# Token runs of 32 in place of 33, seven products in twelve up groups, closing sums given to DMA, and the root chain moved to GpSimd in a fused convolution and MLP kernel

## The chip, the cores and the metric

One core of one Trainium2 chip. The metric is device time in microseconds (us). Each kernel was run several times, and medians are quoted. All runs used here are of the fast state: their granted clocks are given where they matter. The result was measured in one session (the record does not name its chip) and the experiments on three other chips; in the four places the kernel before took 992.5, 996.2, 995.7 and 995.4 us. So kernels are compared by their ratio to the kernel before on the same chip, not by their microseconds.

## The reference

Softmax weights over 7 taps and 8 heads make a causal depthwise convolution, and its result y goes through a layer norm without shift, a product up to 768 features, a ReLU, a product down to 192, and a residual addition. All is float32.

```python
# x: (8, 4224, 192); weight: (8 heads, 7 taps); w_ch1: (192, 768); w_ch2: (768, 192)
w = softmax(weight, axis=-1)
y[b, s, h, :] = sum_k w[h, k] * x_padded[b, s + k, h, :]        # causal, 24 channels a head
yn = (y - mean(y)) / sqrt(var(y) + 1e-06) * g_ln
out = y + maximum(yn @ w_ch1, 0.0) @ w_ch2
```

## The kernel before

Tokens lie on the 128 partitions in *runs*: 33 tokens of one batch entry per partition. A *group* is some columns of these runs (17 and 16 alternately, 6 to 12 in the first entry). Per group, ScalarE and DVE convolve, DVE transposes, TensorE multiplies up and down in 32x32 tiles, and the output is transposed back, scaled by the root (1/sqrt of the variance) on ScalarE, and added to y in HBM by an accumulating DMA. The *down* product uses seven products for eight quarters (as in Strassen's scheme) from the fourth group on; the *up* product does so only in the groups of 16 (`MIXED`).

```python
    R = S // P                        # 33 tokens a run
    J = 17
    ...
    groups = []
    for b in range(B):
        j0 = 0
        for n in (6, 7, 8, R - 21) if b == 0 else (J - 1, J):
            groups.append((b, j0, n))
            j0 += n
    MIXED = range(6, NG, 2)           # six groups, all of 16
    ...
    def root(g):                      # 16 operations, all on DVE
        nc.vector.tensor_tensor(d, st[:, 0:n, 1], st[:, 0:n, 4], op=ALU.subtract)
        nc.vector.tensor_tensor(v, st[:, 0:n, 2], st[:, 0:n, 5], op=ALU.add)
        ...
        for _ in range(3):
            nc.vector.tensor_tensor(d, r, r, op=ALU.mult)
            ...
    def sums_of_y(g):                 # the four sums that the seven products of the up need
        nc.vector.tensor_tensor(s1, a21, a22, op=ALU.add)
        nc.vector.tensor_tensor(s2, s1, a11, op=ALU.subtract)
        nc.vector.tensor_tensor(s3, a21, a11, op=ALU.subtract)
        nc.vector.tensor_tensor(s4, a12, s2, op=ALU.subtract)
    ...
    def down_fast(g):                 # ends like this
        product(0, a[:, 1, 1], w2sums[:, 1], c21, False)
        some_taps(taps_behind[4])     # taps of group g+2 on ScalarE, then y += tb by DMA
        product(0, a[:, 0, 0], w2sums[:, 0], parts[1], False)
        some_taps(taps_behind[5])
        product(0, a[:, 0, 1], b[3], c12, False)
    ...
    def finish_fast(g, half, flat, cs, parts):
        fresh = cs[:, CH * half : CH * half + CH, 1]
        nc.vector.tensor_tensor(fresh, fresh, parts[half], op=ALU.add)      # closing sum, DVE
        for c in range(CH * half, CH * half + CH):
            nc.vector.transpose(ot[:, 0:n, C * c : C * c + C], ...)
    ...
        parts = down_fast(g)
        for half in range(last, 2):
            finish_fast(g, half, *parts)
        ...
        if g + 1 in MIXED:
            sums_of_y(g + 1)
```

## Time and profile before

| | before |
|---|---|
| median of device time | 992.5 us |
| span of the profile, granted clock | 992.1 us, 1.00 |
| busy: TensorE, DVE, ScalarE, GpSimd | 99, 89, 59, 8% |
| GpSimd's DMA queue, share of 16 engines | 34.2% |
| first large product starts | 25.9 us |

The prediction below shows the main lines of the page (the profiler's summary of a run), TensorE's timeline and the stretches. Two more places are needed later. First DVE's timeline at the end of a down (start, duration, engine, line, operation): the closing sums, L790, and behind each the three transposes of its half (of the second half, two are shown).

```profile
562.53 0.95 DVE L790 TENSOR_TENSOR cs<-cs,part 128x768 f32<-128x768 f32 x1
563.52 1.90 DVE L792 STREAM_TRANSPOSE ot<-cs 128x512 f32<-128x512 f32 x3
565.34 0.92 DVE L790 TENSOR_TENSOR cs<-cs,ht 128x768 f32<-128x768 f32 x1
566.36 1.31 DVE L792 STREAM_TRANSPOSE ot<-cs 128x512 f32<-128x512 f32 x2
```

None of these rows shows an idle time in brackets: nothing is waited for here, and the sums cost DVE 1.9 us a group. Second, the head of ScalarE's timeline, where the load of the second group is waited for, briefly (brackets: idle before, and what ended it).

```profile
20.43 0.76 ACT L367 ACTIVATE y<-xg,taps 128x168 f32<-128x168 f32 x2 [0.45 <-DMA xg<-in_x_dram]
```

### The profile page before, as it was taken

The numbers are of one execution on the slowest core, as the hardware profiler recorded it, in microseconds if no ns is written. First come the engines' busy times: TensorE is split into PE (matmuls) and PEld (weight loads), VectorE is DVE, ScalarE is ACT, GpSimd is POOL, SyncE is SP. The second block draws the span as 40 slices with busy tenths as digits, with TensorE's granted clock in tenths as the row PEclk, the third lists the DMA queues.
The fourth block names the chain that finished last, engine by engine and source line by source line (L and its number), as shares of the span: only waits on it lengthen the run. The fifth ranks groups of instructions, "written<-read, shape, count | busy, mean of one in ns | idle before, by whom it ended". The sixth has DMA issues, their size and how long they took to land.

```text
span 992.1 us, 37342 instructions
## 1 busy us (share of the span) xinstructions
PE 979.3 (99%) x16914; PEld 701.4 (71%) x16914; DVE 886.4 (89%) x1622; ACT 588.9 (59%) x1243; POOL 81.5 (8%) x110
## 2 busy tenths in 40 slices
PE   7999999999999999999999999999999999999997
PEld 5888675578585775858767686666857678585786
DVE  6999998899999998998899988999989999899507
ACT  6536464646577565765658566575666746574451
POOL 2001101000010000101001101010000100010000
PEclk9999999999999999999999999999999999999999
DMA  6254727633738354563636735377273854444031
GB/s 196 90 190 75 207 35 219 195 79 60 227 60 229 92 149 136 101 214 70 213 70 118 224 71 188 76 175 193 38 225 68 213 124 101 98 82 74 2 66 70
DMA packets 18702, 126.88 MB, mean 128 GB/s; under 512 B 2415, under 2 KB 3183, under 8 KB 13678
## 3 DMA queue, kind: packets, MB, share of 16 engines
q0 software_dynamic: 12096, 66.75, 34.2%
q1 hardware_dynamic: 6142, 57.73, 15.1%
q8 instruction: 132, 2.16, 0.9%
q14 instruction: 28, 0.23, 0.1%
q10 hardware_dynamic: 304, 0.00, 0.0%
HBM read 38.95 MB, written 50.23 MB: 90 GB/s over the span
## 4 chain that ended last, share of the span: by engine, by line
PE 94%; issue 2%; DMA 2%; DVE 1%; ACT 0%; SPq 0%; POOL 0%; ACTq 0%; DVEq 0%; POOLq 0%
PE ps L520 48%; PE ps L724 39%; PE ps L671 5%; DMA ht<-parts 1%; DMA room<-in_moe_w_ch_dram 1%; DVE ht L689 1%; PE ps L300 1%; PE ps L325 0%; PE ps L330 0%; ACT parts L596 0%; DVE y L829 0%; PE ps L309 0%; PE ps L312 0%; DVE room L225 0%; DVE room L217 0%
## 5 line engine op out<-in xcount | busy, mean ns | idle before, releaser
L520 PE MATMUL ps<-yt,w 32*128 32x256 f32 (+6 forms) x6624 | 426.6, 412 | 0.6 <-ACT parts L596 0.5
L520 PEld LDWEIGHTS ps<-yt,w 32*128 32x128 f32 x6624 | 331.4, 185 | 91.9 <-issue 52.2
L394 DVE SCALAR_TENSOR_TENSOR y<-xg,taps,y 128x408 f32<-128x408 f32 (+5 forms) x734 | 365.9, 575 | 14.6 <-DMA y<-tb 8.6
L724 PE MATMUL ps<-ht,w2sums 128*32 128x256 f32 (+2 forms) x4320 | 236.9, 377 | 0.0
L689 DVE TENSOR_TENSOR ht<-ht 128x1088 f32<-128x1088 f32 (+2 forms) x162 | 184.5, 1208 | 54.5 <-ACT part L730 26.8
L724 PEld LDWEIGHTS ps<-ht,w2sums 128*32 128x32 f32 x4320 | 140.4, 110 | 90.9
L724 PE MATMUL ps<-ht,w 128*32 128x256 f32 (+2 forms) x3240 | 182.6, 378 | 0.2 <-issue 0.2
L508 ACT ACTIVATE ht<-ps 128x256 f32<-128x256 f32 (+2 forms) x312 | 100.9, 409 | 95.6 <-PE ps L520 95.6
L724 PEld LDWEIGHTS ps<-ht,w 128*32 128x32 f32 x3240 | 103.8, 110 | 74.6 <-ACT ot L817 4.6
L730 ACT COPY cs<-ps 128x256 f32<-128x256 f32 (+2 forms) x180 | 65.1, 371 | 120.0 <-PE ps L724 120.0
L510 ACT ACTIVATE ht<-ps 128x2048 f32<-128x2048 f32 (+5 forms) x48 | 63.4, 1320 | 65.0 <-PE ps L520 65.0
L817 ACT ACTIVATE ot<-ot,r 128x192 f32<-128x192 f32 x247 | 94.6, 458 | 4.9 <-DVE ot L792 4.9
L367 ACT ACTIVATE y<-xg,taps 128x408 f32<-128x408 f32 (+5 forms) x137 | 70.5, 588 | 5.9 <-DVE st L421 5.3
L421 DVE BATCH_NORM_STATS2 st<-y 128x6 f32<-128x192 f32 x264 | 70.0, 341 | 0.0
L792 DVE STREAM_TRANSPOSE ot<-cs 128x512 f32<-128x512 f32 (+2 forms) x90 | 58.3, 686 | 8.3 <-ACT cs L730 6.3
L380 ACT ACTIVATE tb<-xg,taps 128x384 f32<-128x384 f32 (+1 forms) x112 | 60.8, 616 | 0.0
L821 POOL DMA_DIRECT2D out_dram<-ot x34 | 31.6, 945 | 347.3 <-ACT ht L508 178.6
L405 DVE STREAM_TRANSPOSE yt<-y 128x3072 f32<-128x3072 f32 (+5 forms) x19 | 56.2, 2957 | 1.9
L671 PE MATMUL ps<-ht,w 128*32 128x192 f32 (+3 forms) x1152 | 51.4, 339 | 0.0
L520 PE MATMUL ps<-ysums,w1sums 32*128 32x256 f32 x864 | 47.7, 374 | 0.0
L671 PEld LDWEIGHTS ps<-ht,w 128*32 128x32 f32 x1152 | 37.1, 110 | 13.7 <-issue 0.5
L383 POOL DMA_DIRECT2D y<-tb x28 | 24.9, 1050 | 264.4 <-ACT cs L730 141.5
(104 smaller groups left out, 499.6 us busy)
## 6 DMA issues: line engine op xcount, KB each, us to landing
y<-tb POOLq DMA_DIRECT2D x21, 768.0 KB, 6.1
out_dram<-ot POOLq DMA_DIRECT2D x20, 768.0 KB, 6.7
xg<-in_x_dram SPq DMA_DIRECT2D x6, 2208.0 KB, 16.1
xg<-in_x_dram SPq DMA_DIRECT2D x6, 2112.0 KB, 12.5
out_dram<-y SPq DMA_DIRECT2D x6, 1632.0 KB, 6.5
out_dram<-y SPq DMA_DIRECT2D x6, 1536.0 KB, 8.0
ht<-parts POOLq DMA_DIRECT2D x6, 1024.0 KB, 7.6
y<-tb POOLq DMA_DIRECT2D x7, 864.0 KB, 10.9
```

What stands on the lines that cost most here:

```text
L367: nc.scalar.mul(dst, src, tap)
L380: nc.scalar.mul(tb[g][:, 0:n, cs], xg[g][:, 1 : 1 + n, cs], taps[:, h, 1:2])
L394: nc.vector.scalar_tensor_tensor(out=y[g][:, 0:n, cs], in0=t[:, k : k + n, cs], scalar=taps[:, h, k : k + 1], in1=y[g][:, 0:n, cs], op0=AL ...
L421: nc.vector.bn_stats(out=sums[g][:, j, :], in_=y[g][:, j, :])
L508: nc.scalar.activation(dst[:, q], src[:, q], AF.Relu)
L510: nc.scalar.activation(dst, src, AF.Relu)
L520: nc.tensor.matmul(banks[:, q, i * w : i * w + w], right[rows, c, P * i : P * i + P], left[rows, :, c, :], start=(first and c == 0 and i = ...
L671: nc.tensor.matmul(bank[C * q : C * q + C, 0:w], w2[:, f, C * c : C * c + C], t[:, f, q, js.start - fast[g] : js.stop - fast[g], :], start ...
L689: nc.vector.tensor_tensor(a[:, *dst, f], a[:, *left, f], a[:, *right, f], op=op)
L724: nc.tensor.matmul(dst[C * q : C * q + C, 0:w], right[:, f, C * c : C * c + C], left[:, f, q], start=(first and f == 0), stop=(f == FC - 1 ...
L730: nc.scalar.copy(to[:, c], dst[:, 0:w].rearrange("p (j t) -> p j t", t=t))
L817: nc.scalar.mul(ots[g][:, j, :], ots[g][:, j, :], rstd[g][:, j : j + 1])
```

## The change

The intent is to use the seven products in the up of twelve groups rather than six (matmuls are the bound), which needs groups of 16 and so runs of 32 tokens. The 128 tokens that remain at each sequence end become one group of 8, loaded as eight small transfers. DVE is relieved to make room: the closing sums of the down become accumulating DMAs in GpSimd's queue, the late product of the up as well, and the root chain goes to GpSimd. The four sums of y become a generator, so that they can be placed between other work: the first two after the transposes of the first half, the third after those of the second.

```diff
-    R = S // P
-    J = 17
+    J = 16
+    R = 2 * J
+    LEFT = (S - P * R) * B // P
...
+    groups = [(0, 0, 6), (None, 0, LEFT), (0, 6, J - 5), (0, J + 1, J - 1)]
+    groups += [(b, j0, J) for b in range(1, B) for j0 in (0, J)]
-    MIXED = range(6, NG, 2)
+    MIXED = range(5, NG - 1)
...
+        if b is None:                          # the group of 8: one transfer a batch entry
+            for b in range(B):
+                queue.dma_start(out=flat[LP * b : LP * b + LP, ...], in_=...)
...
-        nc.vector.tensor_tensor(d, st[:, 0:n, 1], st[:, 0:n, 4], op=ALU.subtract)
+        nc.gpsimd.tensor_tensor(d, st[:, 0:n, 1], st[:, 0:n, 4], op=ALU.subtract)
...  # the whole root chain, 19 operations on GpSimd in place of 16 on DVE
+        def close_by_dma(c, part):
+            add_by_dma(*(v.rearrange("p c j t -> p c (j t)") for v in (c, part)))
...
         product(0, a[:, 1, 1], w2sums[:, 1], c21, False)
+        if g in MIXED:
+            close_by_dma(c21, parts[0])
         some_taps(taps_behind[4])
         product(0, a[:, 0, 0], w2sums[:, 0], parts[1], False)
+        if g in MIXED:
+            close_by_dma(c22, parts[1])
...
-        fresh = cs[:, CH * half : CH * half + CH, 1]
-        nc.vector.tensor_tensor(fresh, fresh, parts[half], op=ALU.add)
+        if g not in MIXED:
+            fresh = cs[:, CH * half : CH * half + CH, 1]
+            nc.vector.tensor_tensor(fresh, fresh, parts[half], op=ALU.add)
...
+        later = sums_of_y(g + 1) if g + 1 in MIXED else iter(())
+        if not last:
+            finish_fast(g, 0, *parts)
+            next(later, None)              # s1 and s2
+        finish_fast(g, 1, *parts)
+        next(later, None)                  # s3; the fourth follows inside the up
```

The order of the products inside the up changed too (the full-width products go last), and so did the places of scalings and convolution steps. Line numbers move: L520, L724, L790 and L792 of before are L532, L734, L802 and L806 of after.

## The prediction

> **What bounds the kernel now.** I read the page's busy shares first, then the TensorE timeline, then the stretches of two groups, then the DMA issues.
>
> ```profile
> span 992.1 us, 37342 instructions
> PE 979.3 (99%) x16914; PEld 701.4 (71%) x16914; DVE 886.4 (89%) x1622; ACT 588.9 (59%) x1243; POOL 81.5 (8%) x110
> ...
> PE 94%; issue 2%; DMA 2%; DVE 1%; ACT 0%; SPq 0%; POOL 0%; ACTq 0%; DVEq 0%; POOLq 0%
> ```
>
> TensorE is busy 99% and is 94% of the chain that ended last, so the kernel lasts as long as its matmuls, and only matmuls removed, or new gaps between them, move the time. DVE at 89% is close behind and must be priced too. The timeline (start, duration) of one batch entry, a group of 17 runs with the plain first matmul and then one of 16 with seven products in it:
>
> ```profile
> 449.32 33.28 PE L520 MATMUL ps<-yt,w 32*128 32x256 f32 x576
> ...
> 511.55 10.61 PE L520 MATMUL ps<-yt,w 32*128 32x512 f32 x144
> 521.99 7.95 PE L520 MATMUL ps<-ysums,w1sums 32*128 32x256 f32 x144
> ...
> 567.52 33.28 PE L520 MATMUL ps<-yt,w 32*128 32x256 f32 x576
> ```
>
> No row in between shows an idle gap. From start to start: plain up (17 runs) 33.2 us, its down 29.0, seven-product up (16 runs) 28.64, its down 27.33; 118.2 us per batch entry. Other engines in the same four stretches (columns: PE, PEld, DVE, ACT, POOL busy, clock, DMA share, GB/s):
>
> ```profile
> 449.32:482.54 33.22, 33.22 (x580) 29.43 (x577) 30.14 (x69) 19.32 (x61) 1.95 (x3) 1.00 0.41 75
> 482.54:511.55 29.01, 29.01 (x508) 16.27 (x505) 25.82 (x39) 16.06 (x37) 2.15 (x3) 1.00 0.72 211
> 511.55:540.19 28.64, 28.64 (x436) 22.04 (x432) 26.87 (x43) 22.17 (x25) 3.51 (x4) 1.00 0.46 85
> 540.19:567.52 27.33, 27.33 (x508) 16.28 (x504) 26.68 (x35) 18.41 (x38) 2.42 (x3) 1.00 0.66 200
> ```
>
> The DMA share averages 0.56 over these 118 us. That has room, but the change fills it.
>
> **What the Trainium skill says.** "GPSIMD Engine Reference", section "Performance versus the Vector engine": GpSimd takes about twice DVE's time for a two-input elementwise operation (4497 against 2293 ns at 2048 elements). The trace before has no such operation on GpSimd, so it neither agrees nor not; its 128x128 memsets take about 0.2 us. "SBUF — State Buffer", section "Who interferes with whom": a DVE instruction with two SBUF inputs and a GpSimd instruction that reads SBUF block each other for a whole instruction. No run yet shows it here. "DMA: Bandwidth & Descriptors", section "Two DMAs through the same engine are not ordered": within one queue descriptors start in order. The trace agrees: three GpSimd transfers issued at 649.5, 650.4 and 651.0 us (512, 512, 768 KB) land 4.7, 7.1 and 11.2 us after their issues, each behind the one ahead, at some 190 GB/s in all.
>
> **The change part by part.**
>
> TensorE. One pass at 256 columns costs 15.75/288 = 54.7 ns, at 512 columns 31.12/288 = 108.1 ns: 1.3 ns plus 0.2086 ns a column. The new order on TensorE is known from the build: groups of 6, 8, 11, 15, 16, then twelve of 16 with seven products, then the last of 16 as 11 plus 5. A new seven-product up has the same matmuls as now (336 passes of 256 and 96 of 512), only in another order. So:
> - 6 runs: 13.04 + 11.84 = 24.9 (as now)
> - 8 runs: 15.75 + 15.68 = 31.4
> - 11 runs: 2 x 288 x 74.7 ns = 43.0
> - 15 runs: 288 x 101.4 ns + 504 x 50.9 ns = 54.8
> - 16 plain: 31.12 + 27.33 = 58.5
> - twelve of 16: 12 x 55.97 = 671.6
> - last: 288 x (74.7 + 34.7) ns + 504 x 37.5 ns + 9.96 = 60.4
>
> Sum 944.6. Before the first of these lie 25.9 us (weights), after the last matmul 5.2 us. Total **975.7 us**, 16.4 us or 1.65% less than the span. That is the ceiling of the gain and it already falls short of 2%: six more groups save about 3.2 us each, and the runs split off as a group of 8 and the less even early groups take a little back.
>
> DVE, per seven-product group of 16, from busy time over count in the groups table: 40 convolution steps x 0.534 = 21.3; transpose of y 3.4; 16 moments x 0.265 = 4.2; 12 sums on the hidden tile 13.9; 3 additions from PSUM 1.1; 6 transposes out 3.9; 4 sums of y 3.8. Sum 51.6 of 56.0 us, 92%. Gone per group: the addition of the late product (2.4), the closing sums (1.9) and, every other group, the root chain (16 x 0.2 = 3.2). So DVE alone does not become the bound, but it has only 4.4 us per group to lose.
>
> ScalarE: 7 evictions and 2 plain ones x 1.88, 2 ReLUs x 1.9, 16 scalings x 0.38, 18 copies x 0.36, 16 taps x 0.54 = 42 of 56 us. In the up part it holds about 27 of 28.6 us, as it does now with 14 scalings.
>
> DMA, per group: 1 MB three times (was one and two halves in every other group), 384 KB twice (new), taps and output 1.5 MB each, all accumulating, 7.1 MB at about 197 GB/s = 36 us; loading x and storing y 3.7 MB at about 370 GB/s = 10 us. Together 46 of 56 us, **82% against 56%**. This is the part that can turn the gain back.
>
> GpSimd: 19 small operations per two groups, estimated at 0.3 us each from the 0.2 us memsets plus a wait, some 6 us, in the last 3 us of a down and the first few of the next up. First use is the scaling about 10 us into that up. Not on the path if the estimate holds.
>
> Head: x of the second group now comes in 8 transfers of 16 partitions. SyncE issues take about 0.45 us each, and ScalarE waits 0.45 us for this load already; its convolution on DVE is 1.2 us longer than for 7 runs while DVE was ready only 0.8 us early. About +1 us.
>
> **The wait I expect.** Take a down's start as zero. The fifth product is evicted at 20.1, its closing transfer goes out then; the taps end at 21.2 and their two 768 KB transfers follow; the sixth product is evicted at 23.9 and its closing transfer goes out last in the same queue. The trace has such a pair of 768 KB moving data for 8.2 us:
>
> ```profile
> y<-tb POOLq DMA_DIRECT2D x2, 768.0 KB, 8.2
> ```
>
> So 384 + 1536 + 384 KB from 21.4 end near 33.5 and land near 34, which is 6.7 us into the next up. DVE then has the second half's three transposes (2.0) and, behind them in its order, the third sum of y (0.95), ready at about 9.7. TensorE wants that sum for its fourth product at 3 x 2.59 = 7.8. That is **2 us of TensorE idle** at each of the 11 boundaries between seven-product groups, 22 us in all. I give this a half chance: the landing has to come only 2 us sooner for it to vanish, and the code looks as though its author had placed the sums around these waits. Half of 22 is 11: 975.7 + 1 + 11, about **987 us** on the clock of the medians.
>
> **Rivals.** (a) All is hidden; TensorE stays gapless and the time is 976 to 978. For it: 99% busy now, and the one gap of the trace before is 0.53 us. Against it: the queue above. (b) The boundary wait is real and about 2 to 3 us: 997 to 1008, so the whole gain is lost or more. For it: the arithmetic of the queue. (c) The reuse of one buffer inside an up: the first 1 MB transfer must land before the sixth product is evicted, 15.6 us into the up, and goes out at 7.2; 7.6 us of landing is its median, 9.2 its worst, so 1 us is to spare. If GpSimd's root chain is slowed by DVE's two-input operations to 0.7 us an operation, the transfer goes out late at every other group, ScalarE stands, and TensorE loses 2 to 4 us six times: another 12 to 24 us. For it: the port rule. Against it: DVE waits for a transfer, not computing, for much of that time. (d) DVE becomes the bound through the lower sum, which waits for the third 1 MB transfer (landing estimated at 28 us into an up) and leaves under 1 us before the hidden sums are due; 2 us later would cost up to 2 us a group.
>
> **Range and chances.** (a) about 0.4, (b) with or without parts of (c) and (d) about 0.5, worse about 0.1. The range is 975 to 1006. Faster by over 2% means under 972.6, below the TensorE sum: 0.05. Slower by over 2% means above 1012.3: needs over 3 us of idle at every boundary: 0.08. Within 2%: 0.87.
>
> **What would show each step.** TensorE: rows of the seven-product groups 28.6 and 27.3 us long; if start to start exceeds 56 us, the surplus is idle time. Boundary wait: TensorE idle ahead of the matmuls on ysums and w1sums released by DVE, and DVE idle ahead of its output transposes released by the small closing DMA; neither there means (a). Buffer reuse: ScalarE idle ahead of evictions into parts, released by DMA. GpSimd: duration from the chain's first to last operation near 6 us. DMA share near 0.8 in mid-kernel. The prediction is wrong if TensorE's own time per pass changes, if GpSimd's chain takes over 12 us, or if the closing transfers overtake the taps' transfers.

## The result

The changed kernel takes 1041.5 us (1040.7 to 1042.9, 4 runs) against 992.5: **4.9% slower**, where half a per cent faster had been predicted; ratio 1.0494 with a 95% interval of 1.0476 to 1.0512. Ratios here are the mean time of one kernel's fast runs over that of the other's of the same rounds, so not quite the ratio of the quoted medians. The result is outside the predicted range of 975 to 1006 us, and 54 us over the predicted time.

The page of the changed kernel:

```profile
span 1041.2 us, 35698 instructions
PE 987.3 (95%) x16050; PEld 690.0 (66%) x16050; DVE 842.5 (81%) x1465; ACT 625.1 (60%) x1034; POOL 188.6 (18%) x329
...
q0 software_dynamic: 24256, 100.97, 50.6%
...
PE 55%; issue 17%; DMA 14%; DVE 7%; POOL 4%; ACT 1%; POOLq 0%; DVEq 0%; ACTq 0%
```

TensorE has 5% fewer instructions and yet 8 us more busy time, which is a first hint at its clock. Its share of the chain that ended last fell from 94 to 55%; DMA has 14%. DVE was indeed relieved, from 89 to 81%. GpSimd's queue moves half as much again, 101 against 67 MB.

TensorE's timeline over one boundary between two seven-product groups (the down ends and the up starts at 545.67):

```profile
545.67 5.46 PE L532 MATMUL ps<-yt,w 32*128 32x256 f32 x96
550.96 2.77 PE L532 MATMUL ps<-ysums,w1sums 32*128 32x256 f32 x48
557.07 7.15 PE L532 MATMUL ps<-ysums,w1sums 32*128 32x256 f32 x96 [3.35 <-DVE ysums L584]
564.02 2.80 PE L532 MATMUL ps<-yt,w1sums 32*128 32x256 f32 x48
```

Two things are to be seen. Ahead of the fourth product TensorE idles 3.35 us for L584, the third sum of y on DVE. And the 96 passes after it take 7.15 us, where 96 passes of the same shape took 5.46 at the top. The other engines at the same place:

```profile
538.70 1.28 POOL L590 DMA_DIRECT2D cs<-part  x1 [15.14 <-ACT cs L740]
539.72 2.08 POOL L403 DMA_DIRECT2D y<-tb  x2
...
542.59 1.27 POOL L590 DMA_DIRECT2D cs<-room  x1 [0.78 <-ACT room L740]
...
554.19 1.90 DVE L806 STREAM_TRANSPOSE ot<-cs 128x512 f32<-128x512 f32 x3 [7.13 <-DMA cs<-room]
...
556.01 0.92 DVE L584 TENSOR_TENSOR ysums<-yt 128x768 f32<-128x768 f32 x1
```

The second closing transfer, `cs<-room`, is issued at 542.59 behind the two tap transfers of 768 KB; DVE idles 7.13 us for it, transposes, and only then computes the sum that TensorE wants. (Of the twelve such waits of DVE the profile puts seven down to this transfer and five to ScalarE's eviction into `parts_tb`, which ends at the same time, at 554.07 here. e9 below parts the two: there the transfer lands early, and at one boundary DVE transposes at 554.37, where that eviction starts only at 562.54.) The waits, summed over the kernel (engine, operand, line <- releaser: us, times, longest):

```profile
PE ps L532 <- DVE ysums L584: 37.8, 11, 3.8
```

The DMA issues (KB each, median us from issue to landing) show what the place in the queue does; the first of the two equal closing transfers goes ahead of the taps, the second behind them:

```profile
y<-tb POOLq DMA_DIRECT2D x28, 768.0 KB, 9.5
...
cs<-part POOLq DMA_DIRECT2D x12, 384.0 KB, 4.4
cs<-room POOLq DMA_DIRECT2D x12, 384.0 KB, 11.5
```

Stretches around the same boundary (columns: PE, PEld, DVE, ACT and POOL busy, granted clock, DMA share, GB/s; in short stretches the share can come out above 1). The last row is a narrower cut of the first two, from 557.30 to 560.70 us:

```profile
557.07:559.00 1.93, 1.93 (x20) 1.93 (x24) 1.93 (x5) 0.00 (x0) 0.00 (x0) 0.56 1.17 242
559.00:561.00 2.00, 2.00 (x26) 2.00 (x25) 2.00 (x5) 0.00 (x0) 0.00 (x0) 0.57 0.81 164
561.00:563.00 2.00, 2.00 (x44) 2.00 (x43) 2.00 (x4) 1.31 (x1) 0.00 (x0) 1.00 0.03 8
...
557.30:560.70 3.40, 3.40 (x36) 3.40 (x36) 3.40 (x8) 0.00 (x0) 0.00 (x0) 0.50 0.94 193
```

The 0.56 and 0.57 are means over stretches in which the clock changes. The narrower cut has exactly 0.50, and cut into steps of 0.1 us the trace has 0.50 from 557.29 to 560.70, which is 3.41 us, and 1.00 on both sides. The kernel before has 1.00 from its first matmul to its last. At half the clock for 3.41 us, 1.7 us of work is lost, which explains 7.15 us in place of 5.46. One of the eleven boundaries, the first, is spared although its idle time is among the longest:

```profile
313.27 5.46 PE L532 MATMUL ps<-ysums,w1sums 32*128 32x256 f32 x96 [3.67 <-DVE ysums L584]
```

The Trainium skill, "TensorE: Matmul & The Clock Gate", section "What's actually happening", says that an idle window of about 3.4 us takes the clock to half, that about 3.4 us of sustained work bring it back, and that the window runs freely. The trace agrees in the half, in the 3.41 us and in the free running; how idle a window must be is taken up at the end.

The head, ScalarE's timeline:

```profile
26.40 0.80 ACT L387 ACTIVATE y<-xg,taps 128x192 f32<-128x192 f32 x2 [4.83 <-DMA xg<-in_x_dram]
```

The second group's eight small loads land late, ScalarE waits 4.83 us for them (0.45 before), its next work, the evictions of the weights, is late, and the first large product starts at 31.06 rather than 25.90 us.

The account, on the predicted sum of TensorE, head and tail:

| | us |
|---|---|
| predicted sum, no idle time | 975.7 |
| head, 31.06 − 25.90 | 5.2 |
| wait ahead of the second group's up | 0.7 |
| 11 boundaries: the twelve seven-product groups take 730.16 (244.90 to 975.06) less the predicted 671.6 | 58.5 |
| sum, against a span of 1041.2 | 1040.1 |

That is 5.32 us a boundary. At the boundary shown, 3.52 are the wait (the fourth product starts 6.11 us after the third, where 2.59 is a product's time without a wait) and 1.77 the slow clock (the next two products take 6.95 from start to start, where two of 2.59 are due).

### The profile page after: what moved, and what is told of

Its sections match the earlier page's. It is cut to its first block, busy times and chain, and to the rows that moved or that the text cites. A ratio compares the mean times of both kernels' runs of the same rounds, so it can differ in the third digit from the quotient of the medians.

```text
span 1041.2 us, 35698 instructions
## 1 busy us (share of the span) xinstructions
PE 987.3 (95%) x16050; PEld 690.0 (66%) x16050; DVE 842.5 (81%) x1465; ACT 625.1 (60%) x1034; POOL 188.6 (18%) x329
## 4 chain that ended last, share of the span: by engine, by line
PE 55%; issue 17%; DMA 14%; DVE 7%; POOL 4%; ACT 1%; POOLq 0%; DVEq 0%; ACTq 0%
PE ps L532 30%; PE ps L734 21%; DMA cs<-room 9%; PE ps L681 4%; DVE y L414 2%; DMA y<-tb 2%; DVE room L699 2%; DVE ot L806 1%; POOL y L403 1%; DMA raw<-in_moe_w_ch_dram 1%; POOL room L590 1%; DVE ysums L584 1%; DMA gb<-in_moe_g_ln_dram 1%; DMA xg<-in_x_dram 1%; POOL out_dram L838 1%
## 5 line engine op out<-in xcount | busy, mean ns | idle before, releaser
L414 DVE SCALAR_TENSOR_TENSOR y<-xg,taps,y 128x384 f32<-128x384 f32 (+4 forms) x734 | 368.2, 578 | 3.5 <-issue 3.4
L532 PE MATMUL ps<-yt,w 32*128 32x512 f32 (+5 forms) x4320 | 334.3, 461 | 1.1 <-DVE yt L425 0.7
L532 PEld LDWEIGHTS ps<-yt,w 32*128 32x128 f32 x4320 | 221.0, 185 | 106.6 <-issue 88.9
L734 PE MATMUL ps<-room,w2sums 128*32 128x256 f32 (+2 forms) x4320 | 233.5, 374 | 0.5 <-DVE room L699 0.3
L734 PEld LDWEIGHTS ps<-room,w2sums 128*32 128x32 f32 x4320 | 140.9, 110 | 87.7 <-DVE room L699 2.6
L699 DVE TENSOR_TENSOR room<-room 128x1024 f32<-128x1024 f32 (+2 forms) x144 | 160.4, 1184 | 41.6 <-ACT part L740 23.2
L734 PE MATMUL ps<-room,w 128*32 128x256 f32 (+2 forms) x3240 | 179.3, 374 | 0.0
L734 PEld LDWEIGHTS ps<-room,w 128*32 128x32 f32 x3240 | 104.6, 110 | 72.9 <-ACT ot L831 9.1
L532 PE MATMUL ps<-ysums,w1sums 32*128 32x256 f32 x1728 | 115.3, 423 | 37.8 <-DVE ysums L584 37.8
L532 PEld LDWEIGHTS ps<-ysums,w1sums 32*128 32x128 f32 x1728 | 106.7, 212 | 44.2 <-ACT ot L831 41.9
L806 DVE STREAM_TRANSPOSE ot<-cs 128x512 f32<-128x512 f32 (+2 forms) x90 | 55.8, 670 | 77.4 <-DMA cs<-room 41.7
L522 ACT ACTIVATE room<-ps 128x2048 f32<-128x2048 f32 (+4 forms) x54 | 79.7, 1475 | 54.9 <-PE ps L532 54.8
L708 DVE SCALAR_TENSOR_TENSOR room<-room 128x1024 f32<-128x1024 f32 x36 | 43.0, 1223 | 43.6 <-DMA room<-parts_tb 22.6
## 6 DMA issues: line engine op xcount, KB each, us to landing
cs<-room POOLq DMA_DIRECT2D x12, 384.0 KB, 11.5
```

Of the source, the lines that this page charges most:

```text
L414: nc.vector.scalar_tensor_tensor(out=y[g][:, 0:n, cs], in0=t[:, k : k + n, cs], scalar=taps[:, h, k : k + 1], in1=y[g][:, 0:n, cs], op0=AL ...
L522: nc.scalar.activation(dst, src, AF.Relu)
L532: nc.tensor.matmul(banks[:, q, i * w : i * w + w], right[rows, c, P * i : P * i + P], left[rows, :, c, :], start=(first and c == 0 and i = ...
L699: nc.vector.tensor_tensor(a[:, *dst, f], a[:, *left, f], a[:, *right, f], op=op)
L734: nc.tensor.matmul(dst[C * q : C * q + C, 0:w], right[:, f, C * c : C * c + C], left[:, f, q], start=(first and f == 0), stop=(f == FC - 1 ...
L806: nc.vector.transpose(ot[:, 0:n, C * c : C * c + C], flat[:, c].rearrange("p (j t) -> p j t", t=C))
```

## The experiments

The theory: the fourth product of each seven-product up waits for the landing of the second closing transfer, because DVE's order puts the transposes that need that transfer ahead of the third sum; the wait then lowers TensorE's clock. Rivals: the root chain on GpSimd, by its port conflict with DVE, delays things; DMA as a whole is too full; the regrouping itself costs; the loading order of the head explains the rest.

| run | closing sums | other edit | ratio to before | 95% interval |
|---|---|---|---|---|
| c1, the changed kernel again | DMA | none | 1.0482 | 1.0465 to 1.0500 |
| e1 | DMA | third sum ahead of the transposes | 0.9998 | 0.9990 to 1.0007 |
| e2 | DVE | none | 0.9899 | 0.9883 to 0.9916 |
| e4 | DMA | TensorE kept busy in the wait | 1.0317 | 1.0302 to 1.0332 |
| e5 | DMA | order of loads | 1.0451 | 1.0435 to 1.0466 |
| e9 | DMA | taps' transfers behind the closing ones | 1.0614 | 1.0598 to 1.0630 |
| e10 | DVE | seven products in six groups only | 1.0056 | 1.0041 to 1.0071 |
| e7 | DVE | second group loaded by GpSimd's queue | 0.9921 | 0.9906 to 0.9936 |
| e3 | DMA | root chain on DVE | 1.0472 | 1.0454 to 1.0491 |
| e12 | DVE | root chain on DVE | 0.9909 | 0.9886 to 0.9933 |
| c2, e2 again | DVE | none | 0.9904 | 0.9885 to 0.9922 |
| e11 | DVE | first tap of the second group on DVE | 0.9871 | 0.9854 to 0.9887 |

All results were correct, and all profiled runs are of the fast state. The diffs are against the changed kernel. e1, e2, e4 and e5 shared one chip, c1, e7, e9 and e10 another, e3, e11, e12 and c2 a third.

**c1: the changed kernel again.**

> The changed kernel as it is, so that the other three of this call are compared on one chip. Ratio to before 1.049, as measured on the first chip; every theory expects the same.

It gave 1.0482, the result again within the intervals, on another chip. Here too ten of the eleven boundaries have slow passes; the one that has none is the last, with 3.27 us of idle time.

**e1: the third sum first.** The wait stays where it is, but the sum no longer stands behind it.

```diff
             finish_fast(g, 0, *parts)
             next(later, None)
+            next(later, None)
         finish_fast(g, 1, *parts)
-        next(later, None)
```

> Only the order on DVE changes: the third sum of y goes ahead of the second half's three transposes. Theory W (TensorE's 3.4 us idle at each of 11 boundaries is the wait of that sum behind a small closing transfer, and the 96 passes after it, 7.15 us instead of 5.35, are slow only because the clock drops after the idle time): both go, 11 x (3.4 + 1.8) = 57 us. What stays is a shorter wait for the first eviction into the shared buffer, which waits for the taps' transfers until 6.4 us into the up and ends at 8.4, while TensorE wants the bank at 7.8: 11 x 0.6, perhaps 1 with what follows. So about 995 us (984 to 1000), clock back to 0.995 or more. Rival D (DVE or the DMA engines are the real bound, at 81% busy and 66% share): the idle time moves to another product, and the time stays above 1020.

It gave 996.1 us, 0.9998. One moved operation, with the same instructions and transfers, takes back 4.8%; e2 below is a further hundredth faster on the same chip. DVE still idles 6.24 us for its transposes, which now costs TensorE nothing. TensorE's timeline shows what remains:

```profile
482.18 5.46 PE L532 MATMUL ps<-ysums,w1sums 32*128 32x256 f32 x96 [1.96 <-ACT parts_tb L613]
```

ScalarE's eviction into `parts_tb` waits for the tap transfers (`y<-tb`) that read the same buffer; the longest such idle time is 1.96 us, and all twelve sum to 7.0 us. So part of the wait by a fuller queue would have been there anyway, though it is much smaller. The 96 passes take 5.46 us again: this idle time of 1.96 us did not lower the clock.

**e2: the closing sums back on DVE.**

```diff
-        if g in MIXED:
-            close_by_dma(c21, parts[0])
...
-        if g in MIXED:
-            close_by_dma(c22, parts[1])
...
-        if g not in MIXED:
-            fresh = cs[:, CH * half : CH * half + CH, 1]
-            nc.vector.tensor_tensor(fresh, fresh, parts[half], op=ALU.add)
+        fresh = cs[:, CH * half : CH * half + CH, 1]
+        nc.vector.tensor_tensor(fresh, fresh, parts[half], op=ALU.add)
```

> One part of the change undone in the twelve groups: the two closing sums of the second matmul by DVE (as before), not by accumulating transfers. Theory W: DVE then waits only for ScalarE's copies, its third sum is ready about 5.5 us into the up where TensorE wants it at 7.8, so the idle time and the slow clock go; the taps' transfers also lone in the queue and land 2 us sooner. About 986 us (980 to 995) although DVE works 1.9 us more per group. Rival D (DVE too full): adding 12 x 1.9 us to DVE leaves the time above 1030.

It gave 986.1 us, 0.9899. DVE and TensorE at a boundary:

```profile
527.97 0.95 DVE L799 TENSOR_TENSOR cs<-cs,room 128x768 f32<-128x768 f32 x1
529.03 1.90 DVE L801 STREAM_TRANSPOSE ot<-cs 128x512 f32<-128x512 f32 x3
530.85 0.92 DVE L584 TENSOR_TENSOR ysums<-yt 128x768 f32<-128x768 f32 x1
```

```profile
526.16 5.46 PE L532 MATMUL ps<-yt,w 32*128 32x256 f32 x96
531.45 7.95 PE L532 MATMUL ps<-ysums,w1sums 32*128 32x256 f32 x144
...
582.14 5.46 PE L532 MATMUL ps<-yt,w 32*128 32x256 f32 x96
```

The third sum is ready at 531.8, well before the fourth product needs it, the three products in one row of 144 passes have no gap, and from group to group it is 55.98 us: the predicted 55.97. DVE is 88% busy and still keeps up. So this one part, 1.9 us of DVE work per group moved to the DMA, costs 1.0482 − 0.9899 = 5.8 hundredths of the time before, or 58 us, which is what the account has for the 11 boundaries.

**e4: TensorE kept busy in the wait.** Six matmuls into a bank that the next product overwrites; the wait on DVE remains.

```diff
+        if g > MIXED[0]:
+            for _ in range(6):
+                nc.tensor.matmul(
+                    other[:, 0, 0:256], w1[:, 0, 0:P], w1[:, 1, 0:256], start=True, stop=True
+                )
         rows_of_tiles(other, s3, w1sums[:, 2], True, False)
```

> Six idle-time matmuls (about 2.6 us, result overwritten) are put on TensorE ahead of the fourth product of each seven-product group but the first; nothing else moves, DVE's sum still comes late. Theory W with a clock part: the wait stays but TensorE isn't idle, the clock stays at full speed, the 96 passes take 5.35 instead of 7.15 us: 1041.5 - 11 x 1.8 = about 1022 us. If the slow passes had another cause (contention with the transfers that start then), the time stays at 1041 or rises.

It gave 1027.7 us, 1.0317: less slow than the changed kernel by 1.65 hundredths, some 16 us, though TensorE has more to do.

```profile
371.37 2.86 PE L640 MATMUL ps<-w 128*128 128x256 f32 x12 [0.70 <-ACT parts_tb L613]
374.16 5.46 PE L532 MATMUL ps<-ysums,w1sums 32*128 32x256 f32 x96
```

The useless matmuls (L640) fill the wait, and the 96 passes after it take 5.46 us at all 11 boundaries, not 7.15. That shows that the slow passes come of the idle time. The rival, that the transfers which start then slow them, is answered too: they still run beside these passes (a DMA share of 0.73 from 374.16 to 379.50 us), with a clock of 1.00. The expectation of 1022 was meant on the first chip, a ratio of about 1.030, so it was nearly met; the filler hardly lengthened the wait, since at ten of the 11 boundaries the sum is ready less than 0.1 us before the product starts.

**e9: the taps' transfers behind the closing ones.** If the second closing transfer is late because it stands behind 1.5 MB in one queue, it must land early when it stands ahead.

```diff
-        if heads[1] == H:
-            for j1, j2 in ((0, n // 2), (n // 2, n)):
-                nc.gpsimd.dma_start(out=y[g]..., in_=tb[g]..., accum_op=ALU.add)
+        if heads[1] == H and g - 2 not in MIXED:
+            add_taps(g)
...
             close_by_dma(c22, parts[1])
+            if g + 2 < NG:
+                add_taps(g + 2)
```

> Only the order in GpSimd's queue changes: in the twelve groups the two 768 KB transfers of the taps go out behind the second closing transfer, not ahead of it. Theory Q (the closing transfer takes 11.5 us only because 1.5 MB stand ahead of it in the queue): it lands some 4.4 us after its issue, as the first closing transfer does, DVE's sum is in time, and the 3.4 us of idle time go. The taps land about 2.5 us later, so the eviction that reuses their buffer is late and TensorE waits up to 2 us there: about 1.8 us at 11 boundaries, ratio 1.00 to 1.02. Rival (such a small accumulating transfer is slow at that moment whatever stands ahead, for example because ScalarE or DVE are busy): its landing stays near 11 us and the ratio near 1.049.

```profile
cs<-room POOLq DMA_DIRECT2D x12, 384.0 KB, 4.6
```

It lands in 4.6 us rather than 11.5: the queue is what made it late, not its size and not DMA load as a whole. DVE's waits for it, 5.6 to 7.2 us in the changed kernel, shrink to at most 1.5. But the time is 1.0614, worse than before the edit, where 1.00 to 1.02 was expected:

```profile
564.46 7.15 PE L536 MATMUL ps<-ysums,w1sums 32*128 32x256 f32 x96 [3.96 <-ACT parts_tb L617]
```

Now the taps' transfers come some 4 us later, ScalarE waits for their buffer, and TensorE for ScalarE: 47.5 us in all over 11 boundaries, again with the slow clock. The queue has two users with a deadline in the first 8 us of the up, and it can serve only one first. I had taken the slack of the second one to be larger.

**e10: seven products in six groups only.** e2's edit, and the regrouped kernel with as many seven-product ups as before.

```diff
-    MIXED = range(5, NG - 1)
+    MIXED = range(6, NG - 1, 2)
```

> The new runs of 32 tokens and groups of 16, closing sums on DVE, but seven products in the first matmul of only every other group (6 groups, as before the change). It tells what the regrouping is worth alone. Theory: a plain up of 16 runs is 31.12 us and a seven-product one 28.64, so 6 x 2.48 = 15 us more than the same kernel with twelve, ratio 0.990 + 0.015 = 1.005: the regrouping alone gains nothing, it only lets six more groups have seven products. Rival (part of the gain comes from somewhere else, such as the root chain on GpSimd): ratio under 1.000.

It gave 1.0056 as expected. So the new groups alone cost about half a per cent, all of it in the head (first large product at 32.88 us, 7.0 later than in the kernel before), and six more seven-product ups bring 1.0056 − 0.9899, some 15.6 us or 2.6 us each; the prediction had 3.2, though its own row times give 31.12 − 28.64 = 2.48.

**e5: the load of the second group ahead of the weights.**

```diff
     load_x(0)
+    load_x(1)
     nc.sync.dma_start(out=raw2..., in_=w2_words...)
-    load_x(1)
```

> Only the head: x of the second group (8 transfers of 16 partitions) is issued ahead of the second matmul's weights, so that none of the 8 waits for the landing of those weights. Theory: the last of the 8 goes out at 19.05 us because it waits for the weights' landing, lands at 26.3 and holds ScalarE 4.8 us; issued first it goes out by about 13 and lands near 20, so the first big matmul starts at about 26.5 instead of 31.1: 1041.5 - 4.5 = 1037 us. Rival: the 8 transfers are slow by themselves (16 partitions each), then nothing is gained.

The ratio is 1.0451, some 3 us better than c1's on another chip, with intervals that just touch. The first large product starts at 28.76 us, 2.3 sooner than in the changed kernel but not at 26.5: the first group's own load now lands later. Right in direction, and half of what was expected; the boundary waits are as they were (37.5 us).

**e7: that load from GpSimd's queue, on top of e2.**

```diff
+    load_x(1, nc.gpsimd)      # at the end of GpSimd's own start-up work; removed from SyncE
```

> Two repairs: the closing sums of the second matmul by DVE, as in the run that gave 0.990, and the 8 transfers that load x of the second group issued from GpSimd's queue instead of SyncE's, after its constants are made. Theory (those 8 wait on SyncE for earlier transfers to land, so they come late and hold ScalarE): from GpSimd they go out between 8 and 16 us, land near 20, and the first big matmul starts near 26 us instead of 31: ratio 0.985 (977 of 992 us). Rival (the 8 transfers are slow by themselves or slow the weights' loads): ratio stays at 0.990.

A miss: 0.9921, no better than e2. Here the first group's load landed in 13.5 us (8.7 in the kernel before), TensorE waited 4.1 us for it, its clock was at half for 10.2 us around that wait (15.7 to 26.0 us), and the first large product started at 34.11 us. Whatever order the loads are given in, they share the start with the weights; moving one delays another.

**e11: no wait of ScalarE for that load, on top of e2.** The first tap of the second group is computed on DVE, after the first group's up has been given to TensorE.

```diff
-        first_tap(1, heads=(0, 2))
...
-                first_tap(1, heads=(2, 4))
...
-            first_tap(1, False, heads=(4, H))
+            first_tap(1, False)       # False: on DVE
```

> Closing sums on DVE as in the earlier run, and the first tap of the second group (the group of 8 with its eight small loads) wholly on DVE and only after the first group's up, so that ScalarE does not stand waiting for that load ahead of the first group's work. Theory (ScalarE, held by the load of the second group, delays the first large matmul from 26 to 31 us): the first large matmul starts near 26 to 27 us, a wait of 1 to 2 us appears ahead of the second group's up, ratio 0.984 to 0.987 where the version without this edit had 0.990. Rival (something else holds the head, for instance the landing of the weights): 0.990 and the same start as before.

```profile
27.12 13.32 PE L530 MATMUL ps<-yt,w 32*128 32x192 f32 x288
...
53.69 15.82 PE L530 MATMUL ps<-yt,w 32*128 32x256 f32 x288 [1.41 <-DVE yt L423]
```

It gave 983.3 us, 0.9871, beside 0.9904 for e2 on the same chip (c2). The first large product starts at 27.12 us (31.72 in c2), the 1.41 us ahead of the second group are the expected price, and the second group starts 3.7 us sooner (57.35 in c2). Its span of 981.4 is 3.2 us shorter than c2's. This shows that ScalarE, held by the load, was the cause in the head. It is the best version found, **1.3% faster than the kernel before**.

**e3 and e12: the root chain back on DVE,** with the closing sums by DMA and on DVE respectively. The edit is the same, the sixteen `nc.vector` operations of the kernel before in place of the nineteen on GpSimd.

```diff
-        nc.gpsimd.tensor_tensor(d, st[:, 0:n, 1], st[:, 0:n, 4], op=ALU.subtract)
+        nc.vector.tensor_tensor(d, st[:, 0:n, 1], st[:, 0:n, 4], op=ALU.subtract)
...
```

> The changed kernel with only the root chain put back on DVE (sixteen operations of about 0.2 us, 3.2 us of DVE per two groups). Theory (the boundary wait is set by the landing of the closing transfer, and GpSimd's chain is off the path): DVE stands idle some 7 us per group ahead of that landing, so the 3.2 us disappear in it; ratio to the kernel before 1.04 to 1.055, as the changed kernel's 1.048. Rival (GpSimd's chain on the port it shares with DVE, or its late scalings, is what costs time): the ratio falls clearly, to 1.03 or less.

> Closing sums on DVE and the root chain on DVE too, so that neither of the two moves off DVE remains and only the regrouping with seven products in twelve groups does. DVE would be busy 88% plus 1.6 us per group, about 91%, in groups of 56 us. If DVE still keeps up: 0.990 as with the chain on GpSimd. If the chain on GpSimd is what makes room on a full DVE: waits of TensorE on DVE of up to 1 us per group appear and the ratio is 0.995 to 1.01.

```profile
496.72 7.15 PE L537 MATMUL ps<-ysums,w1sums 32*128 32x256 f32 x96 [4.20 <-DVE d L451]
...
557.98 7.15 PE L537 MATMUL ps<-ysums,w1sums 32*128 32x256 f32 x96 [3.31 <-DVE ysums L589]
```

e3: 1.0472, as the changed kernel; the waits are 3.1 to 4.2 us as before (the profile puts five of them down to the root chain, which now stands on DVE too), and all 11 are followed by slow passes. e12: 0.9909, with e2's kernel (c2) at 0.9904 on the same chip; DVE at 90% leaves no gap at the boundaries. So the root chain on GpSimd neither causes the loss nor is worth anything measurable; the rival falls, and so does this part of the change's gain.

**c2: e2 again,** the control for e11 and e12.

> Control on this chip: closing sums on DVE, root chain on GpSimd, unchanged from the earlier run. Expected 0.990, TensorE without gaps at the boundaries between seven-product groups.

0.9904, as e2.

## Why the prediction was wrong

The prediction had the change half a per cent faster; it was 4.9% slower. **What mechanism it had, held**: the boundary wait was described before the run, with its releaser (DVE idle ahead of its transposes for the small closing DMA, then the third sum, then TensorE), and TensorE waits for that sum at all 11 boundaries; e1 and e2 each remove this wait. The fuller DMA held: a share of 0.75 over the twelve groups, where 0.82 was predicted and the kernel before has 0.56. TensorE's pass times held at the full clock: group to group 55.98 us in e2 for 55.97, and e11's span of 981.4 is its sum of 975.7 with a head 1.2 us later, 2.9 us of recorded small waits and 1.6 us left over. No version tried gained over 2%, as it said; 1.3% was the most. But one of its own signs of being wrong came true, "if TensorE's own time per pass changes": that is item 2.

What failed are the size of the wait, a term for the clock that was missing, and the size of the head, in this order:

1. **"That is 2 us of TensorE idle at each of the 11 boundaries", taken at "a half chance" for 11 us.** It came at every boundary, at 3.44 us of recorded idle time in the mean, 37.8 us. The step behind it that was off is the landing: "end near 33.5 and land near 34". In the boundary shown, the down starts at 518.34 (545.67 − 27.33), and DVE goes on after the landing at 554.19, which is at 35.9. The issues were right (the second closing transfer goes out at 24.2, where 23.9 had been said) and so, nearly, was the end of the bulk of the data; the tail was not. The DMA row of the stretch from 550 to 554.5 us, in 40 slices of 0.11 us (busy share in tenths):

```profile
DMA  2799999999999999999520100100100100000000
```

   Nearly all data has moved by 552.3 (20 slices), 34.0 on the prediction's clock. Then for 1.4 us the row shows tenths of 0 and 1, a share of 0.08 to 0.10 in finer stretches, where one engine of sixteen would be 0.06, and DVE's transposes start 0.5 us after that. Only GpSimd's queue has packets in this stretch. So the landing came 1.4 us after the time that the mean rate gives. The Trainium skill, "DMA: Bandwidth & Descriptors", section "Latency and other measured facts", says that two of the sixteen DMA engines, 7 and 15, are usually slower than the rest in traces, and puts that, as its best guess, down to the descriptor rings of transfers issued by GpSimd; a trailing share of one or two engines fits that, though the views used here do not tell which engines trailed. The other step that was off is the half chance itself: "the landing has to come only 2 us sooner" was true, but no line that the prediction shows says that it would. With the whole wait as measured, and without item 2, its sum would have been 975.7 + 1 + 37.8 = 1014.5, already out of its range.

2. **A term that was missing: the clock.** Nothing in the sum stood for it, since the kernel before has no idle time over 0.5 us between its large products and always shows 1.00. It cost 1.77 us at each of ten boundaries, 17.7 us, about half of what the wait cost by itself; e4 shows that it is a consequence of the idle time, and in e1 an idle time of 1.96 us did not bring it. It also makes the loss jump: at the predicted 2 us there would have been little or none.

3. **"About +1 us" for the head** was 5.2 us. The prediction priced the eight issues but not that the last of them would go out only at 19.05 us, at the moment when the weights' transfer ahead of them in SyncE's queue landed. That it is ScalarE's wait for this load that moves the first product is shown by e11, not by e5 or e7. The clock has a part here too, which no run isolates: in the changed kernel it is at half from 28.2 to 31.6 us, in the small products just ahead of the first large one, and in e11's head it never is.

**The rivals.** (b) was the right one and too small: 11 × 5.3 is 58 us, where it had 2 to 3 us each; some 0.5 to 1.5 of the difference is the longer wait and the rest the clock. (a), all hidden, is refuted. (c), the GpSimd chain slowed by DVE: the trace has it in small:

```profile
484.41 0.92 POOL L468 TENSOR_TENSOR d<-r 128x32 f32<-128x32 f32 x1
485.41 0.92 POOL L469 TENSOR_TENSOR d<-d,v 128x32 f32<-128x32 f32 x1
...
487.05 0.24 POOL L468 TENSOR_TENSOR d<-r 128x32 f32<-128x32 f32 x1
```

Two of the 19 operations take 0.92 us, exactly while DVE runs its two-input additions of 0.92 and 0.96 us (484.31 to 486.2); the same operation at 487.05 takes 0.24. This agrees with the rule in the Trainium skill, "SBUF — State Buffer", section "Who interferes with whom", that the two block each other for a whole instruction. But the chain as a whole took 7.15 us (482.38 to 489.53) where 6 had been estimated and 12 been set as the mark of a wrong prediction, and e3 and e12 show it is not on the path. The sign given for (c), ScalarE idle for the reuse of a buffer inside an up, cost TensorE 0.4 us once. (d), DVE as the bound, is refuted by e2 and e12, which run DVE at 88 and 90% without gaps at the boundaries; in the changed kernel DVE did wait for the third 1 MB transfer, 22.6 us in twelve groups, but no wait of TensorE for the lower sum is recorded in them.

What stays open: which DMA engines trail the others by 1.4 us and why.

## What to carry to other kernels

When a small transfer is put into a queue that a large one also uses, work out its landing from the whole queue ahead of it plus a tail, and then look at what stands *behind* the wait in the waiting engine's order: here one reordered addition was worth 4.8%, and the relieved engine had not been the bound at all. On a TensorE that never idles, price a new gap of some 3 us at one and a half times its length, because the passes after it may run at half the clock: here 53 of 55 gaps of 3.1 us and more were followed by that, and one of 1.96 us was not. Of several changes made at once, undo each alone: here the one that made the gain (seven products in more groups, 15.6 us) was hidden by one that was meant to help it.

## What the Trainium skill lacked or had wrong

- "TensorE: Matmul & The Clock Gate", section "What's actually happening": its half clock and its freely running window of about 3.4 us are what the traces show (0.50 for 3.41 us; within each run the starts of the slow stretches lie whole multiples of 3.413 us apart). But it speaks of an "idle window" and does not say how idle. Laying that grid over the idle times of the changed kernel, c1, e3, e5, e9 and e1, the windows at full clock with 2.08 us or more of idle time were all followed by half the clock (53 of them), and none with 0.8 to 1.93 us was (31). So a gap shorter than a window was enough (3.10 us in e3), while two longer ones escaped because the grid cut them in two: 3.67 us into 1.93 and 1.74, and in c1 3.27 us into 1.42 and 1.86.
- "DMA: Bandwidth & Descriptors": no figure for how long a small accumulating SBUF transfer takes behind others in GpSimd's queue. Here one of 384 KB landed 4.4 us after its issue ahead of the taps, 4.6 when moved ahead of them (e9), and 11.5 behind their 1.5 MB. The section "Latency and other measured facts" names slower engines but not by how much; here the tail after the bulk had moved was 1.4 us at a share of 0.08 to 0.10.
- "GPSIMD Engine Reference", section "Performance versus the Vector engine": a two-input figure for 2048 elements only, and none as small as here. For 32 elements a partition GpSimd took 0.21 to 0.28 us, near DVE's 0.18 to 0.22 in the kernel before (33 elements), and 0.92 us when DVE's two-input addition ran beside it.
